# Reordering the side jobs of an expert chunk: the place of two weight loads among three float64 pieces

## The chip, the cores and the metric

The kernel runs on one core of a Trainium2 chip. The metric is device time in microseconds (us), the median of several executions.

## What is computed

Three stages follow one another on 2304 tokens with 512 features: windowed attention, a mixture of eight experts whose gate is normalised by rows and columns, and a dense layer pair with a leaky ReLU. The weights `w_in` and `w_out` of the last pair arrive as float64.

```python
scores = np.where(mask, scale * q @ k.T + bias, -1e9)     # 4 x 8 heads, 576 tokens, window 128
x = softmax(scores) @ v                                   # (2304, 512)
P = exp(x @ w_gate - max);  8 times: P /= P.sum(1); P /= P.sum(0); P *= N / E
for e in range(8):                                        # D = 512, F = 1024
    out += P[:, e:e+1] * (np.maximum(x @ w1[e], 0) @ w2[e])
h = out @ w_in                                            # d_ff = 2048, float64 weights
return np.maximum(0.01 * h, h) @ w_out
```

## The kernel before

**Chunks and units.** Each expert's hidden layer is cut into two halves, so there are 16 expert chunks, followed by 4 chunks of the dense pair. A chunk has two weight matrices of 512 x 512, which the code calls factors: `W[0][ci]` (from `w1`) and `W[1][ci]` (from `w2`). A chunk is worked off in five units, one for each group of token tiles, in the order 0, 4, 1, 2, 3. Each matrix product is done with seven block products instead of eight (a Strassen scheme), in float16 parts. In every unit TensorE runs the steps of the first product (`a_steps`, L707, results `s` and `sq`) mixed with those of the second product of the unit before (`b_steps`, L824, results `t`). ScalarE and VectorE empty the PSUM banks: L719 and L731 (ScalarE, to `q`), L723 (VectorE, to `sq`), L755, L761 and L777 (ScalarE, to the float16 `h`), L736 (VectorE), L834 (ScalarE, to `part`), L835 (GpSimd, `part` into `acc`), L837 (VectorE, `t` into `acc`). TensorE can only go on with a bank when the reader of its last content is done.

**Side jobs.** While chunk ci is computed, the factors of chunk ci+1 have to be loaded and prepared. For each factor there is one load of 1 MB (L551, on SP's queue), then `scale()`: four ScalarE passes that find the size of its numbers (`largest`, L555), a short chain over TensorE and VectorE for the scale, four ScalarE passes that apply it (L558); then `early()`: the first two float16 parts (L429 on ScalarE, L430 on GpSimd) and four sums (L582, GpSimd). Besides, the float64 weights of the last stage are turned to float32 in 32 pieces, three of them in each of the expert chunks 1 to 10 and two in chunk 11. A piece is a load of 512 KB (L630), then five jobs: `exponent` (L636 VectorE, L639 ScalarE), `signed` (L642 VectorE), `high` (L647 VectorE, L648 ScalarE), `low` (L654 ScalarE, L656 GpSimd), `put` (L660 GpSimd, then the store L661 on SP's queue).

**What sets the order.** The jobs are functions in the list `side`, filled when unit 4 of a chunk begins (`p == 4`). After each TensorE step `tick` takes one or two from the list's front; a `None` is a step without a job. The number taken is such that the list is empty at the end of the chunk. A scheduler then places the instructions on each engine, where they run in order. All large loads, of factors and pieces, share the tile tag `raw` with two buffers (8 KB in each partition): a load has to wait until the buffer's last user is done, which for a piece is the landing of its store. SP's queue issues in order.

In the job list before, all pieces stand ahead of both factors: load piece 1, load piece 2, piece 1, load piece 3, piece 2, piece 3, load both factors, ten empty steps, `scale` and `early` of the first factor, then of the second.

Of the kernel before, what the change touches and what calls it, by code (L numbers as in the profile page):

```python
# [31 lines left out]
def attn_moe_kernel(  # L32
# [81 lines left out]
    side, gating, inputs = [], [], []  # L114
# [18 lines left out]
    def tick(n=1):  # L133
        for d in due:
            d[0] -= 1
        for d in [d for d in due if d[0] <= 0]:
            due.remove(d)
            d[1]()
        pop(gating)
        pop(inputs)  # L140
        for _ in range(n):
            pop(side)
# [291 lines left out]
    def weigh_pair(ci, p):  # L434
        t0, n = PAIRS[p]
        if ci not in pu:
            pu[ci] = small.tile([P, NTILE], F32, tag="pu", name="pu")
        c = slice(t0, t0 + 2 * n)
        nc.scalar.activation(out=pu[ci][:, c], in_=rxt[0 if ci == 0 else 1][:, c], func=AF.Copy, scale=rw[ci])

    class Inputs:
# [22 lines left out]
        def weigh(self):  # L464
            c = slice(self.t0, self.t0 + 2 * self.n)
            nc.scalar.activation(out=rxt[self.phase][:, c], in_=self.sr[:, 1:2].to_broadcast([P, 2 * self.n]), func=AF.Copy)
            if self.phase == 0:
                weigh_pair(0, self.p)
# [64 lines left out]
    NCE = len(chunks)  # L533
    for c in range(F2 // FC):
        chunks.append((win32[:, c * FC:(c + 1) * FC], wout32[c * FC:(c + 1) * FC, :], None))
    NC = len(chunks)
# [73 lines left out]
    def weights(ci):  # L610
        for which in range(2):
            W[which][ci] = Weights(ci, which)
# [237 lines left out]
    def merge(a, b):  # L850

        if not b:
            return a
        seq = [a[0], b[0], a[1], a[2], b[1]] + a[3:7]
        a, b = a[7:], b[2:]
        tail = b[-3:] if len(b) > 10 else b[-1:]
        b = b[:len(b) - len(tail)]
        na, nb = 0, 0
        while na < len(a) or nb < len(b):
            if nb < len(b) and nb * len(a) <= na * len(b):  # L860
                seq.append(b[nb])
                nb += 1
            else:
                seq.append(a[na])
                na += 1
        return seq + tail
# [93 lines left out]

    cast = list(range(2 * KT * (F2 // FC)))

    def cast_jobs(n):

        todo = [to_single(cast.pop(0)) for _ in range(min(n, len(cast)))]
        jobs = [load for load, _ in todo[:2]] + [None] * 8
        for k, (_, rest) in enumerate(todo):
            jobs += rest + [load for load, _ in todo[k + 2:k + 3]]
        return jobs

    def weight_jobs(ci):
        weights(ci)
        a, b = W[0][ci], W[1][ci]
        return [a.load, b.load] + [None] * 10 + a.scale() + a.early() + b.scale() + b.early()

    def weigh(ci):
        pu[ci] = small.tile([P, NTILE], F32, tag="pu", name="pu")
# [12 lines left out]
    for n, u in enumerate(units + [None]):  # L990
        a, b = [], b_steps(*prev)
        if u is not None:
            ci, p = u
            assert ci < NCE or p in split_pairs
            a = a_steps(ci, p)
            k0 = len(a) - 7
            if p == ends[ci] and ci + 1 < NC:
                a = [[f] + ([lambda j=k - k0: W[0][ci + 1].at(j)] if k >= k0 else []) for k, f in enumerate(a)]
            else:
                a = [[f] for f in a]  # L1000
        if prev[1] == ends[prev[0]] and prev[0] + 1 < NC:
            k0 = len(b) - 7
            b = [[f] + ([lambda j=k - k0: W[1][prev[0] + 1].at(j)] if k >= k0 else []) for k, f in enumerate(b)]
        else:
            b = [[f] for f in b]
        if u is not None and ci >= 1:
            if n and units[n - 1][0] != ci and ci != NCE:
                weigh(ci)
            if p == 4:
                side += cast_jobs(3) if ci < NCE - 1 else []  # L1010
                side += weight_jobs(ci + 1) if ci + 1 < NC else []
        if prev[0] == NCE:
            weigh_pair(*prev)
        seq = merge(a, b) if a else b

        rest = {4: 57, 1: 36, 2: 8, 3: -19}.get(p) if u is not None and ci >= 1 else None
        for k, fs in enumerate(seq):
            for f in fs:
                f()
            if u is not None and ci == 0:  # L1020
                tick(2)
            elif u is None or not side:
                tick()
            elif rest is not None:
                tick(-(-len(side) // max(len(seq) - k + rest, 1)))
            else:
                tick()
        assert u is None or p != 3 or not side
        if prev[0] == NCE - 1:
            inputs += [None] * 6 + Inputs(prev[1], 1).all()  # L1030
        if u == (1, 0):
            assert not any(gating)
        prev = u
# [43 lines left out]
```

## Time and profile before

| | |
|---|---|
| median of 3 runs (lowest, highest) | 2003.38 us (2001.25, 2008.05) |
| profiled execution, first to last instruction | 2015.9 us |
| TensorE busy | 1911.6 us (95%) |
| VectorE, ScalarE, GpSimd busy | 1408.6 us (70%), 1365.7 us (68%), 1319.5 us (65%) |
| mean granted clock of TensorE | 0.984 |

The page gives no other time for the profiled execution than its span, which lies 0.6% above the median of the runs. All places below are counted from the span's start; chunk 7, which is followed closely, runs from about 850 to 940 us. A busy TensorE may still be slow: the granted clock says whether its matmuls run at full speed (1.0) or half (0.5).

### The profile page before, as it was taken

The page shows a single profiled execution, that of the slowest core. Times are in us where ns is not written, and L with a number is a line of the kernel's source. Part 1 is how long each engine was busy: PE and PEld are TensorE (multiplying, and loading weights), DVE is VectorE, ACT ScalarE, POOL GpSimd, SP SyncE. Part 2 cuts the span into 40 slices and gives each one's busy share as a digit, 9 for nine tenths or more (in the row PEclk, how much of TensorE's full clock was granted, in tenths as well). Part 3 has the DMA queues.
Part 4 walks back from the last instruction along what each step waited for, and adds up shares of the span by engine and source line. Part 5 has one row for each costly group of instructions (what it writes and reads, how often), then busy time and mean ns, then how long its engine had stood idle before and what let it go on. Part 6 is the DMA issues. An engine that isn't in the chain of part 4 may idle for free.

```text
span 2015.9 us, 45342 instructions
## 1 busy us (share of the span) xinstructions
PE 1911.6 (95%) x17693; PEld 1654.9 (82%) x17693; DVE 1408.6 (70%) x3881; ACT 1365.7 (68%) x3110; POOL 1319.5 (65%) x1133
## 2 busy tenths in 40 slices
PE   8899988899999989999999999999999998999998
PEld 6677767788888878788887888889898887889897
DVE  5877568666767767676766677666666677677776
ACT  6776685767666666757666675766666678776754
POOL 4632346577685868677685877767657686667743
PEclk9799899999999999999999999999999999999999
DMA  4231000111202021111202021100010000001002
GB/s 126 79 90 48 22 7 22 69 38 58 68 28 80 22 69 38 54 64 38 79 12 79 22 69 54 43 22 30 15 43 23 22 22 22 22 22 43 1 22 74
DMA packets 55271, 88.90 MB, mean 44 GB/s; under 512 B 3344, under 2 KB 21776, under 8 KB 55056
## 3 DMA queue, kind: packets, MB, share of 16 engines
q1 hardware_dynamic: 55056, 86.01, 13.1%
q8 instruction: 138, 2.26, 0.5%
q14 instruction: 77, 0.63, 0.1%
HBM read 72.89 MB, written 13.11 MB: 43 GB/s over the span
## 4 chain that ended last, share of the span: by engine, by line
PE 73%; DVE 9%; ACT 6%; DMA 4%; POOL 4%; issue 3%; SPq 0%; POOLq 0%; ACTq 0%; DVEq 0%
PE t L824 33%; PE s L707 20%; PE sq L707 14%; PE s L234 3%; DMA raw<-in_moe_w_dram 3%; PE o L288 2%; PE pt L273 2%; DVE e L262 1%; DVE acc L837 1%; ACT junk L555 1%; DVE raw L642 1%; POOL h L780 1%; DVE h L736 1%; DVE s L736 1%; POOL acc L835 1%
## 5 line engine op out<-in xcount | busy, mean ns | idle before, releaser
L824 PE MATMUL t<-w,h 128*128 128x256 f16 x7560 | 978.0, 274 | 37.2 <-ACT part L834 14.4
L707 PEld LDWEIGHTS <-w 128*128 128x128 f16 x8400 | 761.0, 98 | 129.5 <-issue 42.5
L824 PEld LDWEIGHTS <-h 128*128 128x128 f16 x7560 | 732.3, 98 | 143.6 <-issue 44.6
L707 PE MATMUL s<-xp,w 128*128 128x256 f16 (+1 forms) x4908 | 618.4, 264 | 34.4 <-ACT q L731 23.3
L837 DVE SCALAR_TENSOR_TENSOR acc<-t,pu,acc 128x256 f32<-128x256 f32 x864 | 406.7, 478 | 238.7 <-PE t L824 193.2
L780 POOL TENSOR_TENSOR h<-s,h 128x1024 f16<-128x1024 f32 x180 | 386.7, 2149 | 181.5 <-ACT h L777 133.6
L707 PE MATMUL sq<-xp,w 128*128 128x256 f16 (+1 forms) x3492 | 439.5, 262 | 2.0 <-ACT q L719 1.0
L835 POOL TENSOR_TENSOR acc<-acc,part 128x256 f32<-128x256 f32 x324 | 242.0, 749 | 240.8 <-ACT part L834 177.0
L430 POOL TENSOR_TENSOR w<-raw,w 128x512 f16<-128x512 f32 x240 | 277.8, 1175 | 46.8 <-ACT w L429 46.5
L736 DVE SCALAR_TENSOR_TENSOR h<-sq,h 128x512 f16<-128x512 f32 (+1 forms) x348 | 190.7, 549 | 68.5 <-ACT h L761 50.8
L834 ACT ACTIVATE part<-t,pu 128x256 f32<-128x256 f32 x324 | 152.7, 471 | 118.7 <-PE t L824 109.1
L777 ACT ACTIVATE h<-s 128x1024 f16<-128x1024 f32 x180 | 190.0, 1055 | 47.1 <-DVE s L736 44.3
L723 DVE SCALAR_TENSOR_TENSOR sq<-sq,q 128x256 f32<-128x256 f32 x348 | 148.4, 427 | 78.2 <-PE sq L707 67.5
L719 ACT ACTIVATE q<-s 128x256 f32<-128x256 f32 x366 | 138.5, 381 | 84.5 <-PE s L707 60.8
L429 ACT ACTIVATE w<-raw 128x512 f16<-128x512 f32 x240 | 147.5, 626 | 15.1 <-PE t L824 7.9
L736 DVE SCALAR_TENSOR_TENSOR s<-sq,s 128x256 f32<-128x256 f32 x348 | 144.1, 414 | 2.6
L755 ACT ACTIVATE h<-sq 128x512 f16<-128x512 f32 x174 | 103.5, 595 | 55.1 <-DVE sq L723 31.9
L736 DVE SCALAR_TENSOR_TENSOR s<-sq,q 128x256 f32<-128x256 f32 x348 | 129.9, 414 | 11.8 <-ACT q L731 9.8
L723 DVE SCALAR_TENSOR_TENSOR sq<-s,q 128x256 f32<-128x256 f32 x174 | 74.6, 429 | 88.5 <-ACT q L719 80.6
L555 ACT ACTIVATE junk<-raw 128x512 bf16<-128x512 f32 x160 | 100.6, 629 | 31.8 <-DMA raw<-in_moe_w_dram 30.9
L558 ACT ACTIVATE raw<-raw,sr 128x512 f32<-128x512 f32 x160 | 102.3, 714 | 1.5 <-DVE sr L424 1.4
L582 POOL TENSOR_TENSOR raw<-raw 128x512 f32<-128x512 f32 x80 | 102.5, 1281 | 0.0
(139 smaller groups left out, 1867.6 us busy)
## 6 DMA issues: line engine op xcount, KB each, us to landing
raw<-in_moe_w_dram SPq DMA_DIRECT2D x32, 1024.0 KB, 5.2
raw<-in_moe_w_in_dram SPq DMA_DIRECT2D x16, 512.0 KB, 3.7
raw<-in_moe_w_out_dram SPq DMA_DIRECT2D x16, 512.0 KB, 3.5
q_t<-in_q_dram SPq DMA_DIRECT2D x18, 256.0 KB, 3.2
k_t<-in_k_dram SPq DMA_DIRECT2D x18, 256.0 KB, 3.0
v_t<-in_v_dram SPq DMA_DIRECT2D x18, 256.0 KB, 2.8
out_dram<-acc SPq DMA_DIRECT2D x18, 256.0 KB, 2.0
win<-raw SPq DMA_DIRECT2D x16, 256.0 KB, 2.4
```

Source lines behind the costliest of these rows:

```text
L429: nc.scalar.activation(out=hi, in_=src, func=AF.Copy)
L430: nc.gpsimd.tensor_tensor(out=lo, in0=src, in1=hi, op=ALU.subtract)
L707: nc.tensor.matmul(d[b][:, f, :], t[:, wp, kk, ft * P:(ft + 1) * P], XP[p][:, o, kk, xp, :], start=(i == 0 and f == 0 and j in FIRST), sto ...
L719: nc.scalar.activation(out=q[:, k], in_=ps, func=AF.Copy, scale=CS)
L723: nc.vector.scalar_tensor_tensor(out=block(k), in0=ps, scalar=CS, in1=q[:, k], op0=ALU.mult, op1=ALU.add)
L736: nc.vector.scalar_tensor_tensor(out=out, in0=in0, scalar=sc, in1=in1, op0=op0, op1=op)
L777: nc.scalar.activation(out=h[:, 3:7, 0, :], in_=d["s"], func=AF.Copy)
L780: nc.gpsimd.tensor_tensor(out=h[:, 3:7, 1, :], in0=d["s"], in1=h[:, 3:7, 0, :], op=ALU.subtract)
L824: nc.tensor.matmul(ps, h[:, o, hp, f, tt * P:(tt + 1) * P], w[:, wp, ft, :], start=(i == 0 and j in FIRST), stop=(i == 5), skip_group_chec ...
L834: nc.scalar.activation(out=part, in_=ps, func=AF.Copy, scale=s)
L835: nc.gpsimd.tensor_tensor(out=dst, in0=dst, in1=part, op=ALU.add)
L837: nc.vector.scalar_tensor_tensor(out=dst, in0=ps, scalar=s, in1=dst, op0=ALU.mult, op1=ALU.add)
```

## The change

`cast_jobs` and `weight_jobs` become one function, `side_jobs`. In a chunk with three pieces its list is: load piece 1, load piece 2, eight empty steps, piece 1, **load first factor**, piece 2, load piece 3, four empty steps, **`scale` of the first factor**, piece 3, **load second factor**, `early` of the first, eight empty steps, `scale` and `early` of the second. The amount of work is the same; the list is two steps longer (85 entries instead of 83). Where there are only two pieces (chunk 11) the second factor is loaded behind the second piece. Where there are none (chunks 12 and on) the list is as before.

```diff
-    def cast_jobs(n):
+    def side_jobs(ci, n):
 
         todo = [to_single(cast.pop(0)) for _ in range(min(n, len(cast)))]
-        jobs = [load for load, _ in todo[:2]] + [None] * 8
-        for k, (_, rest) in enumerate(todo):
-            jobs += rest + [load for load, _ in todo[k + 2:k + 3]]
-        return jobs
-
-    def weight_jobs(ci):
         weights(ci)
         a, b = W[0][ci], W[1][ci]
-        return [a.load, b.load] + [None] * 10 + a.scale() + a.early() + b.scale() + b.early()
+        jobs = [load for load, _ in todo[:2]]
+        if not todo:
+            return [a.load, b.load] + [None] * 10 + a.scale() + a.early() + b.scale() + b.early()
+        jobs += [None] * 8 + todo[0][1] + [a.load]
+        if len(todo) > 1:
+            jobs += todo[1][1]
+        if len(todo) > 2:
+            jobs += [todo[2][0]] + [None] * 4 + a.scale() + todo[2][1] + [b.load] + a.early()
+        else:
+            jobs += [b.load] + [None] * 8 + a.scale() + a.early()
+        return jobs + [None] * 8 + b.scale() + b.early()
...
             if p == 4:
-                side += cast_jobs(3) if ci < NCE - 1 else []
-                side += weight_jobs(ci + 1) if ci + 1 < NC else []
+                side += side_jobs(ci + 1, 3 if ci < NCE - 1 else 0) if ci + 1 < NC else []
```

On SP's queue the eight DMAs of such a chunk stand in this order before: load 1, load 2, store 1, load 3, store 2, first factor, store 3, second factor. In the changed kernel: load 1, load 2, store 1, first factor, store 2, load 3, store 3, second factor.

The order of instructions moves at three places of chunk 7 that matter below. Buffer numbers are part of the names: `raw_11959`, `raw_11961` are pieces 1 and 2 in both kernels; piece 3 is `raw_12097` before and `raw_12138` in the changed kernel; the first factor is `raw_12205` before and `raw_12077` in the changed one.

VectorE, around the last VectorE job of piece 1 (L647), before:

```order
L723 SCALAR_TENSOR_TENSOR sq_11971<-s0_11945,q_11944 128x256
L723 SCALAR_TENSOR_TENSOR sq_12217<-sq_12217,q_12196 128x256
L642 SCALAR_TENSOR_TENSOR raw_11959<-raw_11959,sign_88 128x512
L837 SCALAR_TENSOR_TENSOR acc15_116<-t0_11836,pu_10394,acc15_116 128x256
L736 SCALAR_TENSOR_TENSOR h_11943<-sq_11971,h_11943 128x2x256
L723 SCALAR_TENSOR_TENSOR sq_12008<-sq_12008,q_11944 128x256
L647 TENSOR_SCALAR raw_11959<-raw_11959 128x512
```

The same place of the changed kernel:

```order
L642 SCALAR_TENSOR_TENSOR raw_11959<-raw_11959,sign_88 128x512
L837 SCALAR_TENSOR_TENSOR acc15_116<-t0_11836,pu_10394,acc15_116 128x256
L723 SCALAR_TENSOR_TENSOR sq_11971<-s0_11945,q_11944 128x256
L647 TENSOR_SCALAR raw_11959<-raw_11959 128x512
L723 SCALAR_TENSOR_TENSOR sq_12008<-sq_12008,q_11944 128x256
```

L647 now follows directly on the L723 that closes a block product of unit 4; before, three other instructions stood between the sign job and it.

ScalarE, from the L755 of the first half of unit 1 on, before:

```order
L755 ACTIVATE h_12195<-sq_12217 128x2x256
L648 ACTIVATE raw_11961<-raw_11961,ones_90 128x512
L834 ACTIVATE part_12143<-t1_12136,pu_11680 128x256
L761 ACTIVATE h_12195<-sq_12242 128x256
L731 ACTIVATE q_12196<-s0_12197 128x256
L654 ACTIVATE raw_12097<-raw_12097 128x512
L719 ACTIVATE q_12288<-s0_12289 128x256
L639 ACTIVATE raw_12097<-raw_12097,shift_92 128x512
L834 ACTIVATE part_12164<-t2_12157,pu_11680 128x256
```

The same place of the changed kernel:

```order
L755 ACTIVATE h_12192<-sq_12214 128x2x256
L555 ACTIVATE junk_12181,mxw_11940<-raw_12077 128x512
L834 ACTIVATE part_12147<-t1_12140,pu_11680 128x256
L555 ACTIVATE junk_12190,mxw_11940<-raw_12077 128x512
L555 ACTIVATE junk_12202,mxw_11940<-raw_12077 128x512
L761 ACTIVATE h_12192<-sq_12243 128x256
L731 ACTIVATE q_12193<-s0_12194 128x256
L555 ACTIVATE junk_12212,mxw_11940<-raw_12077 128x512
L719 ACTIVATE q_12302<-s0_12303 128x256
L834 ACTIVATE part_12164<-t2_12157,pu_11680 128x256
```

The four passes over the first factor (L555) now stand here, one of them ahead of the first L834; the jobs of pieces 2 and 3 that stood here have moved ahead and behind.

GpSimd, from the first job of piece 1 on, before:

```order
L656 TENSOR_TENSOR raw_11959<-raw_11959 128x512
L835 TENSOR_TENSOR acc2_103<-acc2_103,part_12093 128x256
L660 TENSOR_TENSOR raw_11959<-raw_11959 128x512
L780 TENSOR_TENSOR h_11943<-s_12070,h_11943 128x4x256
L656 TENSOR_TENSOR raw_11961<-raw_11961 128x512
L835 TENSOR_TENSOR acc1_102<-acc1_102,part_12143 128x256
L660 TENSOR_TENSOR raw_11961<-raw_11961 128x512
L835 TENSOR_TENSOR acc3_104<-acc3_104,part_12164 128x256
L780 TENSOR_TENSOR h_12195<-s_12275,h_12195 128x4x256
L656 TENSOR_TENSOR raw_12097<-raw_12097 128x512
L660 TENSOR_TENSOR raw_12097<-raw_12097 128x512
```

In the changed kernel, from the second job of piece 2 on (in piece 1 the L660 likewise follows directly on its L656):

```order
L656 TENSOR_TENSOR raw_11961<-raw_11961 128x512
L660 TENSOR_TENSOR raw_11961<-raw_11961 128x512
L835 TENSOR_TENSOR acc1_102<-acc1_102,part_12147 128x256
L835 TENSOR_TENSOR acc3_104<-acc3_104,part_12164 128x256
L780 TENSOR_TENSOR h_12192<-s_12286,h_12192 128x4x256
L835 TENSOR_TENSOR acc16_117<-acc16_117,part_12240 128x256
L835 TENSOR_TENSOR acc17_118<-acc17_118,part_12330 128x256
L656 TENSOR_TENSOR raw_12138<-raw_12138 128x512
L780 TENSOR_TENSOR h_12301<-s_12398,h_12301 128x4x256
L660 TENSOR_TENSOR raw_12138<-raw_12138 128x512
```

Pieces 1 and 2 have lost the L835 that stood inside them, and piece 3 stands two L835 later and has an L780 inside.

## Rows read from the trace of the kernel before

**Rows 1.** TensorE groups, 400 to 1205 us: count, busy, mean ns, idle before, releasers.

```profile
L824 PE MATMUL t<-w,h 128*128 128x256 f16 x3408 | 436.0, 274 | 15.3 <-ACT part L834 10.6 <-DVE acc L837 4.3 <-POOL h L780 0.2
L707 PE MATMUL s<-xp,w 128*128 128x256 f16 (+1 forms) x2157 | 272.3, 265 | 21.6 <-ACT q L731 20.3 <-ACT q L719 0.8 <-DVE sq L723 0.4
```

**Rows 2.** Stretches: chunks 2 to 10, and chunk 13, which has no float64 pieces.

```profile
core 0: us, PE busy (x) PEld busy (x) DVE busy (x) ACT busy (x) POOL busy (x), PEclk, DMA share, GB/s
400.00:1205.30 805.30, 768.33 (x7221) 674.97 (x7220) 549.86 (x1388) 541.74 (x1177) 594.45 (x500) 0.99 0.16 51
1361.80:1446.30 84.50, 84.50 (x813) 75.39 (x811) 55.73 (x148) 55.27 (x123) 57.12 (x50) 1.00 0.08 26
```

**Rows 3.** Waits, 300 to 1300 us: in total, times, longest.

```profile
ACT junk L555 <- DMA raw<-in_moe_w_dram: 30.9, 16, 4.4
```

**Rows 4.** Timeline of SP's queue, chunk 7: start, us, DMA issued.

```profile
891.36 0.33 SPq L661 DMA_DIRECT2D wout<-raw  x1
...
900.06 0.33 SPq L661 DMA_DIRECT2D wout<-raw  x1
902.19 0.38 SPq L551 DMA_DIRECT2D raw<-in_moe_w_dram  x1
```

**Rows 5.** Timeline of ScalarE, chunk 7, at five places.

```profile
896.47 0.46 ACT L834 ACTIVATE part<-t,pu 128x256 f32<-128x256 f32 x1
...
904.83 0.47 ACT L834 ACTIVATE part<-t,pu 128x256 f32<-128x256 f32 x1 [0.61 <-PE t L824]
907.20 0.63 ACT L555 ACTIVATE junk<-raw 128x512 bf16<-128x512 f32 x1 [1.90 <-DMA raw<-in_moe_w_dram]
...
908.84 0.37 ACT L731 ACTIVATE q<-s 128x256 f32<-128x256 f32 x1
...
923.26 1.04 ACT L777 ACTIVATE h<-s 128x1024 f16<-128x1024 f32 x1
```

**Rows 6.** Timeline of TensorE, chunk 7; idle time before in brackets.

```profile
895.53 0.81 PE L824 MATMUL t<-w,h 128*128 128x256 f16 x6
896.98 0.81 PE L824 MATMUL t<-w,h 128*128 128x256 f16 x6 [0.64 <-ACT part L834]
...
909.27 2.52 PE L707 MATMUL s<-xp,w 128*128 128x256 f16 x12 [2.25 <-ACT q L731]
```

**Rows 7.** Timeline of TensorE, the same stall in chunks 2 and 4.

```profile
464.25 0.81 PE L824 MATMUL t<-w,h 128*128 128x256 f16 x6 [3.03 <-ACT part L834]
...
726.89 0.81 PE L824 MATMUL t<-w,h 128*128 128x256 f16 x6 [3.28 <-ACT part L834]
```

**Rows 8.** Stretches behind the stall of chunk 7; columns as in rows 2.

```profile
909.27:912.85 3.58, 3.58 (x18) 2.58 (x18) 2.25 (x8) 3.02 (x8) 1.21 (x2) 0.53 0.76 208
917.00:940.00 23.00, 23.00 (x210) 20.02 (x208) 14.54 (x44) 18.64 (x42) 16.99 (x15) 1.00 0.00 1
```

**Rows 9.** Instructions on the tile raw: duration in ns, least, median, most.

```profile
L647 DVE TENSOR_SCALAR raw<-raw x32: 406/410/2214, 339.0 to 1248.6; 128x512 int32<-128x512 int32 x32
L648 ACT ACTIVATE raw<-raw,ones x32: 706/722/733, 340.2 to 1250.2; 128x512 f32<-128x512 int32 x32
L656 POOL TENSOR_TENSOR raw<-raw x32: 1277/1292/1398, 350.0 to 1254.2; 128x512 f32<-128x512 f32 x32
L660 POOL TENSOR_TENSOR raw<-raw x32: 1262/1272/1362, 352.0 to 1255.6; 128x512 f32<-128x512 f32 x32
```

**Rows 10.** Costliest groups of the whole run, from the page.

```profile
L723 DVE SCALAR_TENSOR_TENSOR sq<-sq,q 128x256 f32<-128x256 f32 x348 | 148.4, 427 | 78.2 <-PE sq L707 67.5
L755 ACT ACTIVATE h<-sq 128x512 f16<-128x512 f32 x174 | 103.5, 595 | 55.1 <-DVE sq L723 31.9
L780 POOL TENSOR_TENSOR h<-s,h 128x1024 f16<-128x1024 f32 x180 | 386.7, 2149 | 181.5 <-ACT h L777 133.6
```

**Rows 11.** Timeline of GpSimd, chunk 7, the add of acc17.

```profile
910.54 0.73 POOL L835 TENSOR_TENSOR acc<-acc,part 128x256 f32<-128x256 f32 x1 [3.04 <-PE s L707]
```

**Rows 12.** DMA from issue to landing, us: the loads of L551.

```profile
DMA to landing us min/median/max: 4.9/5.2/10.1
```

## The prediction

> **What bounds the kernel now.** I read the groups of TensorE first, then stretches, then the waits and the timelines of one chunk. In chunks 2 to 10, which take 805.3 us, TensorE is busy for 768.3 us; in chunk 13, which has no float64 pieces, it never idles [rows 2]. So TensorE is the bound, and the nine chunks with three pieces lose 37.0 us to idle time. The reader should see how few causes that has: 21.6 us lie ahead of matmuls into `s`, 20.3 of them until ScalarE's L731, and 15.3 us ahead of matmuls into `t`, 10.6 of them until ScalarE's L834 [rows 1].
>
> Both releasers are ScalarE, which has idle time of its own, so the question is what ScalarE waited for. Its first pass over a new factor (L555) waited 30.9 us for the factor's load, in 16 waits of up to 4.4 us [rows 3]. Chunk 7 shows how this reaches TensorE. ScalarE is through with L834 at 905.3, finds the factor not there and stands until 907.20; two passes and L761 later L731 starts, at 908.84; TensorE has waited 2.25 us for it when it goes on at 909.27 [rows 5, 6]. In chunks 2 and 4 the same late factor shows as an L834, with 3.03 and 3.28 us [rows 7]. I count as the DMA stall of the nine chunks 20.3 + 3.0 + 3.3 = 26.6 us, 3.0 a chunk. The other 10.4 us, 1.15 a chunk, are short waits such as the 0.64 us at 896.98 [rows 6].
>
> Why is the factor late? Its load is issued at 902.19, when the store of piece 2, issued at 900.06, has landed: the store costs 2.1 us, the load 5.0 (to 907.20) [rows 4, 5]. Piece 1's store went out at 891.36 [rows 4], nearly 11 us earlier, but its buffer was given to piece 3.
>
> There is a second loss behind the stall. From 909.27 to 912.85 the granted clock is 0.53 and TensorE needs 3.58 us for 18 matmuls, 199 ns each; later it is 1.00 and 23.0 us hold 210, 110 ns each [rows 8]. These are the levels of 1.2 and 2.4 GHz; before the fall TensorE had stood idle for 2.25 us. Such a spell costs 18 x 89 ns = 1.6 us. Over the nine chunks the mean clock is 0.99, so about 8 us of 805 go this way (4 to 12, given the rounding) [rows 2].
>
> **The change, part by part.** The instructions are the same; the code orders both the work and SP's DMAs anew. I follow chunk 7 and take its times for all nine, since their pattern repeats.
>
> *First factor, earlier load.* It now waits for piece 1's store. When does that go out? L647 of piece 1 stands directly behind the L723 that closes a block product of unit 4. In the changed order 105 matmuls of 256 columns and 24 of 128 lie between that product and the `t0` group that starts at 895.53 [rows 6]; at 110 ns, and half of it, these take 12.9 us, so the product ends at 882.7. Then follow, one behind the other, L723 0.43, L755 0.60 (beside it L647, 0.41), L648 0.72, L656 1.29 and L660 1.27, with nothing between them any more [rows 9, 10]: the store is issued at about 887.1, 4.3 us earlier than now. It lands at 889.2, the factor at 894.2 to 894.4.
>
> *First factor, earlier use.* The first L555 now stands where ScalarE used to do piece 2's L648, ahead of the L834 that ran at 896.47 [rows 5]. The product whose reading that place follows ends 42 matmuls before 895.53, at 890.9; L723 and L755 take 1.0 [rows 10], so ScalarE gets there at about 892. So it still waits for the load, about 2 us as today, but at another place. What is queued behind it: L834, two more passes, L761, L731. L555 runs 894.3 to 894.9 and L834 until 895.4, and TensorE wants L834 only at 895.53 + 6 x 0.11 = 896.2 [rows 6]: no stall, where there are 0.64 us now. Two passes and L761 take 1.64 us as they do at 907.20 [rows 5], so L731 runs 897.0 to 897.4, and TensorE, which wants it at 896.85, loses 0.55; a further pass delays an L719 by about 0.5. That is 1.05 us against 1.15 today. But the load can be slower than the 5.0 us: the median of this line's loads is 5.2 and single ones take more [rows 12]. I take 0.2 a chunk more than today: +1.8 us.
>
> *The old place.* At 905 piece 3 takes the place of the four passes. Its load follows the landing of piece 2's store, and piece 2 has also moved forward, so VectorE and ScalarE find it there. The DMA stall goes: -26.6 us. Cover gone would mean piece 3 late instead, at most the same stall.
>
> *Second factor, later load.* It now waits for piece 3's store, and on GpSimd piece 3 stands behind the L835 of acc17, now at 910.54 [rows 11]. Without the stall and the slow spell this is 3.9 us earlier, 906.6, done at 907.4; L656, one L780 (2.15) and L660 bring it to 912.1 [rows 9, 10], the store to 914.2, the load to 919.4. ScalarE wants it behind an L777 that now begins at 923.26 [rows 5], so at 924.3 - 3.9 = 920.4. That is 1 us to spare, and TensorE does not want the next L719 at once. Bounds: nothing, or, if GpSimd waits for the L777 that feeds its L780, some 2 us a chunk. I take 0.5, nearer to the row: +4.5 us.
>
> *The clock.* Stalls of 2 us and more vanish, so I take 7 of the 8 us back.
>
> *Nothing for the rest.* Chunk 11, with two pieces, and chunk 1, where the gate runs too, I count at nothing, though they have stalls as well; two empty steps hide under TensorE's own work, as the list still ends with the chunk. The other stages keep their order.
>
> Sum: -26.6 + 1.8 + 4.5 - 7.0 = -27.3 us. The profiled execution took 2015.9 and would take 1988.6; it is 0.6% above the median of the runs, and the stalls are in both, so I carry the difference over: 2003.4 - 27.3 = 1976 us.
>
> **A rule on the clock.** The row shows a slow spell behind a stall of 2.25 us [rows 6, 8]. The Trainium skill, "TensorE: Matmul & The Clock Gate", Part 1, says that the hardware judges activity in a window that runs freely, so that how many matmuls are slow differs from run to run. By the rows the term is -7; by the rule it depends on where a gap falls and could be anything from 0 to -8. The trace has both cases only in so far as the mean of 0.99 is less than a spell in each chunk would give.
>
> **The rivals.**
> - *The clock gives nothing back.* The remaining short waits could still meet slow spells. Then the sum is -20.3: 1983 us. What the Trainium skill says of the free-running window ("TensorE: Matmul & The Clock Gate", Part 1) allows this.
> - *The second factor becomes the late one.* If its load lands 3 us later than worked out, ScalarE stands for about 2 us in each chunk; TensorE loses those instead of the 0.5: +13.5 us, and the clock term goes. -26.6 + 1.8 + 18 = -6.8: 1997 us. For it speaks the chain of three GpSimd steps, store and load; against it that ScalarE now gets rid of piece 3 before.
> - *The wait has only moved.* If the first factor lands 2 us later than worked out (896.3), L834 and L731 are late by 1.4 to 2 us and the old stall stands at the new place: about 2003, no change.
> - *Slower.* If piece 1's store goes out no earlier than now, at 891.36, the factor lands at 898.5, 4.2 us later than worked out; TensorE then loses 1.05 + 3.6 = 4.7 us there against the 4.15 of today, and every chunk meets a slow spell: nine times 0.5 + 1.6, less the 8 of today, + 4.5 for the second factor: +15, so 2018 us. It decides from a landing at about 897.3. Against it: the order on VectorE and GpSimd has cleared the way of piece 1.
>
> That the change does nothing is excluded: SP's queue has the factor ahead of store 2.
>
> **How the numbers follow.** I give 0.51 to the forecast (1966 to 1987), 0.12 to the clock's case (1983), 0.15 to the second factor (1997), 0.11 to a wait that only moves (2003), 0.11 to slower (2010 and up). What a measurement here can tell from no change is about 0.3%, 6 us. Faster is forecast, clock's case, and most of the third: 0.76; same 0.13; slower 0.11. The range from 1963 to 2003 leaves out the slower cases and a little below, where all stalls vanish (-37 - 8 = -45 would be 1958).
>
> **What would show it.** In the new profile the wait of TensorE for L731 in chunks 2 to 10 falls from 20.3 us to under 8; store 1 of chunk 7 goes out near 887, the factor's load directly behind it; L555's first wait on its load is about 2 us and ahead of an L834; the second factor's wait is near 0; chunks take 86 to 87 us, not 89.5. I am wrong if piece 1 is not earlier (VectorE's other work may hold its jobs back), or if the second L555 of a chunk waits for more than 2 us.

## The result, and the profile after

The changed kernel takes 1973.56 us (median of 4 runs, 1969.18 to 1977.06), the kernel before 2005.72 us in runs taken beside it: a ratio of 0.983 (95% interval 0.980 to 0.986). The forecast was 1976 us, in a range from 1963 to 2003. The profiled execution has a span of 1975.3 us, 40.6 us less than the one of before.

The groups of TensorE in chunks 2 to 10, which now run from 396.1 to 1168.6 us (against [rows 1]; columns as there):

```profile
L824 PE MATMUL t<-w,h 128*128 128x256 f16 x3408 | 441.4, 273 | 2.9 <-ACT part L834 1.8 <-DVE acc L837 0.9
L707 PE MATMUL s<-xp,w 128*128 128x256 f16 (+1 forms) x2165 | 272.5, 262 | 9.5 <-ACT q L731 8.7 <-DVE sq L723 0.3
L707 PE MATMUL sq<-xp,w 128*128 128x256 f16 (+1 forms) x1620 | 211.5, 262 | 0.7 <-ACT q L719 0.7
```

The same nine chunks, and chunk 13, as stretches (against [rows 2]):

```profile
396.10:1168.60 772.50, 759.34 (x7229) 671.64 (x7227) 547.10 (x1390) 544.54 (x1173) 591.04 (x497) 1.00 0.16 53
1320.30:1403.80 83.50, 83.50 (x804) 74.51 (x802) 54.09 (x146) 54.39 (x121) 57.37 (x49) 1.00 0.08 27
```

The nine chunks take 772.5 us instead of 805.3. Two things make up the 32.8: TensorE's idle time falls from 37.0 to 13.2 us (772.50 - 759.34), and its busy time for the same work from 768.3 to 759.3, because the stretch now runs at a granted clock of 1.00. The other 7.8 us of the span's difference lie outside: 2.7 in chunk 11 (86.1 to 83.4 us), 3.3 in the first 300 us, where nothing was changed, the rest in small pieces. The medians differ by 32.2 us, so some 8 of the 40.6 belong to these two executions and not to the kernels.

ScalarE's waits for a factor's load, in total, times, longest, from 300 to 1270 us (against [rows 3]):

```profile
ACT junk L555 <- DMA raw<-in_moe_w_dram: 40.0, 20, 2.9
```

This is the surprise: they have not become shorter. There were 30.9 us in 16 waits; now there are 40.0 in 20. In the nine chunks the first passes over a first factor wait 20.5 us in 9 waits (20.1 in 8 before), those over a second factor 17.7 in 9 (5.3 in 5 before). What TensorE loses and what ScalarE waits for have come apart. Chunk 7 shows how. It begins at 828.0 instead of 850.3, so 22.3 us are to be added to compare a place with before.

SP's queue in chunk 7 (against [rows 4]):

```profile
864.35 0.33 SPq L661 DMA_DIRECT2D wout<-raw  x1
866.42 0.38 SPq L551 DMA_DIRECT2D raw<-in_moe_w_dram  x1
...
890.52 0.33 SPq L661 DMA_DIRECT2D wout<-raw  x1
892.59 0.38 SPq L551 DMA_DIRECT2D raw<-in_moe_w_dram  x1
```

ScalarE at the two places where a factor is first used, in the brackets the idle time before (against [rows 5]):

```profile
871.51 0.63 ACT L555 ACTIVATE junk<-raw 128x512 bf16<-128x512 f32 x1 [2.28 <-DMA raw<-in_moe_w_dram]
...
872.14 0.46 ACT L834 ACTIVATE part<-t,pu 128x256 f32<-128x256 f32 x1
...
874.13 0.37 ACT L731 ACTIVATE q<-s 128x256 f32<-128x256 f32 x1
...
895.15 1.05 ACT L777 ACTIVATE h<-s 128x1024 f16<-128x1024 f32 x1
897.65 0.63 ACT L555 ACTIVATE junk<-raw 128x512 bf16<-128x512 f32 x1 [1.46 <-DMA raw<-in_moe_w_dram]
```

TensorE at the same two places (against [rows 6]):

```profile
872.06 1.47 PE L824 MATMUL t<-w,h 128*128 128x256 f16 x12
874.55 1.70 PE L707 MATMUL s<-xp,w 128*128 128x256 f16 x12 [1.02 <-ACT q L731]
...
897.24 0.82 PE L707 MATMUL sq<-xp,w 128*128 128x256 f16 x6
897.89 0.27 PE L707 MATMUL s<-xp,w 128*128 128x256 f16 x1
```

ScalarE stands 2.28 us for the first factor, a little longer than the 1.90 of before, but TensorE has other products in hand meanwhile and loses 1.02 us where it lost 2.25. At the second factor ScalarE stands 1.46 us and TensorE has no idle time at all. The other chunks agree. The gaps of TensorE that end within 3.3 us of the start of a first factor's late pass add up to 22.3 us before and to 9.4 now; behind the second factor's they are 0.3 and 0.7 us.

One long stall is left, in chunk 1: there ScalarE waits for the load of a float64 piece with an L834 right behind it, and TensorE loses 3.04 us, after which the granted clock is 0.50 from 366.1 to 371.0. ScalarE there:

```profile
365.01 0.67 ACT L654 ACTIVATE raw<-raw 128x512 f32<-128x512 uint32 x1 [2.79 <-DMA raw<-in_moe_w_in_dram]
365.58 0.45 ACT L834 ACTIVATE part<-t,pu 128x256 f32<-128x256 f32 x1
```

and TensorE:

```profile
366.09 1.44 PE L824 MATMUL t<-w,h 128*128 128x256 f16 x6 [3.04 <-ACT part L834]
```

### The profile page after: what moved, and what is told of

It is laid out like the page before. It is cut to its first block, busy times and chain, and to the rows that moved or that the text cites. A ratio compares the mean times of both kernels' runs of the same rounds, so it can differ in the third digit from the quotient of the medians.

```text
span 1975.3 us, 45321 instructions
## 1 busy us (share of the span) xinstructions
PE 1899.9 (96%) x17693; PEld 1650.3 (84%) x17693; DVE 1401.9 (71%) x3881; ACT 1370.4 (69%) x3110; POOL 1320.1 (67%) x1133
## 4 chain that ended last, share of the span: by engine, by line
PE 75%; DVE 7%; ACT 6%; DMA 5%; POOL 4%; issue 2%; SPq 0%; POOLq 0%; ACTq 0%; DVEq 0%
PE t L824 34%; PE s L707 20%; PE sq L707 14%; DMA raw<-in_moe_w_dram 3%; PE s L234 3%; PE o L288 2%; PE pt L273 2%; DVE e L262 1%; ACT junk L555 1%; POOL h L780 1%; DVE s L736 1%; POOL w L430 1%; ACT raw L558 1%; DVE acc L837 1%; ACT e L250 1%
## 5 line engine op out<-in xcount | busy, mean ns | idle before, releaser
L837 DVE SCALAR_TENSOR_TENSOR acc<-t,pu,acc 128x256 f32<-128x256 f32 x864 | 407.1, 478 | 219.5 <-PE t L824 168.7
L780 POOL TENSOR_TENSOR h<-s,h 128x1024 f16<-128x1024 f32 x180 | 388.5, 2158 | 132.3 <-ACT h L777 92.8
L707 PE MATMUL sq<-xp,w 128*128 128x256 f16 (+1 forms) x3492 | 446.8, 262 | 3.3 <-ACT q L719 1.7
L835 POOL TENSOR_TENSOR acc<-acc,part 128x256 f32<-128x256 f32 x324 | 236.3, 731 | 284.5 <-ACT part L834 246.9
L834 ACT ACTIVATE part<-t,pu 128x256 f32<-128x256 f32 x324 | 152.9, 472 | 110.5 <-PE t L824 102.0
L777 ACT ACTIVATE h<-s 128x1024 f16<-128x1024 f32 x180 | 189.6, 1053 | 43.0 <-DVE s L736 41.7
L723 DVE SCALAR_TENSOR_TENSOR sq<-sq,q 128x256 f32<-128x256 f32 x348 | 148.2, 426 | 64.5 <-PE sq L707 52.1
L719 ACT ACTIVATE q<-s 128x256 f32<-128x256 f32 x366 | 138.7, 380 | 71.3 <-PE s L707 58.4
L755 ACT ACTIVATE h<-sq 128x512 f16<-128x512 f32 x174 | 103.2, 593 | 59.0 <-PE t L824 28.7
L723 DVE SCALAR_TENSOR_TENSOR sq<-s,q 128x256 f32<-128x256 f32 x174 | 74.4, 428 | 81.7 <-ACT q L719 76.7
L555 ACT ACTIVATE junk<-raw 128x512 bf16<-128x512 f32 x160 | 100.2, 626 | 41.1 <-DMA raw<-in_moe_w_dram 40.0
L761 ACT ACTIVATE h<-sq 128x256 f16<-128x256 f32 x174 | 66.1, 380 | 66.4 <-DVE sq L723 59.4
```

Source lines behind the costliest of these rows:

```text
L707: nc.tensor.matmul(d[b][:, f, :], t[:, wp, kk, ft * P:(ft + 1) * P], XP[p][:, o, kk, xp, :], start=(i == 0 and f == 0 and j in FIRST), sto ...
L719: nc.scalar.activation(out=q[:, k], in_=ps, func=AF.Copy, scale=CS)
L723: nc.vector.scalar_tensor_tensor(out=block(k), in0=ps, scalar=CS, in1=q[:, k], op0=ALU.mult, op1=ALU.add)
L777: nc.scalar.activation(out=h[:, 3:7, 0, :], in_=d["s"], func=AF.Copy)
L780: nc.gpsimd.tensor_tensor(out=h[:, 3:7, 1, :], in0=d["s"], in1=h[:, 3:7, 0, :], op=ALU.subtract)
L834: nc.scalar.activation(out=part, in_=ps, func=AF.Copy, scale=s)
```

## The experiments

Twelve kernels were run. In the first expectations A is the theory that the earlier load brings the gain, B its rival; from the fifth on each says anew what its letters stand for. All ratios are to the kernel before, run beside each.

**The load alone, in the list.** The first factor is loaded behind piece 1 as in the change, but stays in the list where it was scaled before.

```diff
         if len(todo) > 2:
-            jobs += [todo[2][0]] + [None] * 4 + a.scale() + todo[2][1] + [b.load] + a.early()
-        else:
-            jobs += [b.load] + [None] * 8 + a.scale() + a.early()
-        return jobs + [None] * 8 + b.scale() + b.early()
+            jobs += [todo[2][0]] + todo[2][1]
+        return jobs + [b.load] + [None] * 10 + a.scale() + a.early() + b.scale() + b.early()
```

> One part of the change alone: the first factor is loaded behind piece 1 (so it waits for store 1), but it is scaled behind piece 3 and ten empty steps, as before. Theory A (the gain comes from which store the load waits for): the first pass over the first factor waits 0, TensorE's idle time in chunks 2 to 10 falls from 37 to about 15 us (1.15 a chunk that were there anyway, 0.5 for two passes ahead of L731), the slow-clock spells go: 1970 to 1980 us, like the changed kernel. Rival B (the gain comes from scaling the first factor early, which spreads the work of ScalarE and GpSimd): idle stays above 30 us, 1995 to 2005 us.

Measured: 2005.86 us, 1.001 (0.999 to 1.003). This edit gives nothing. A fell; of B the idle time held (37.3 us), the time lies a little above its range. But the run does not show the load alone. In its chunk 7 the scheduler has drawn the four passes ahead of piece 3, although the list has them behind it: the first pass stands 48.4 us behind the start of a chunk (median of the nine), against 56.9 in the kernel before and 43.9 in the change. So the passes are early here too, and piece 3, whose load now stands behind the factor's, is the late one. ScalarE's timeline at its first pass:

```profile
890.02 0.63 ACT L555 ACTIVATE junk<-raw 128x512 bf16<-128x512 f32 x1 [1.62 <-DMA raw<-in_moe_w_dram]
```

VectorE's at the first job of piece 3:

```profile
897.27 0.43 DVE L636 TENSOR_SCALAR raw<-raw 128x512 int32<-128x512 int32 x1 [2.05 <-DMA raw<-in_moe_w_out_dram]
```

TensorE's behind that:

```profile
898.48 0.22 PE L404 MATMUL mt<-identb,e 128*1 128x128 bf16 x1 [1.36 <-DVE acc L837]
900.38 1.44 PE L824 MATMUL t<-w,h 128*128 128x256 f16 x6 [1.68 <-ACT part L834]
```

VectorE waits 2.05 us for piece 3 with an L837 behind; TensorE wants that L837, then an L834, and loses 1.36 + 1.68 = 3.04 us, as much as a chunk of before lost to the factor. The prediction had this as "Cover gone would mean piece 3 late instead, at most the same stall".

**The place alone, in the list.** The change, with the loads of piece 3 and of the first factor exchanged, so that SP's order is that of before.

```diff
-        jobs += [None] * 8 + todo[0][1] + [a.load]
+        jobs += [None] * 8 + todo[0][1] + ([todo[2][0]] if len(todo) > 2 else [a.load])
...
-            jobs += [todo[2][0]] + [None] * 4 + a.scale() + todo[2][1] + [b.load] + a.early()
+            jobs += [a.load] + [None] * 4 + a.scale() + todo[2][1] + [b.load] + a.early()
```

> The changed kernel with two entries of the list exchanged: the load of piece 3 stands behind piece 1, and that of the first factor behind piece 2, so that it waits for store 2 again; all else, with the early scaling, is as in the changed kernel. Theory A: the factor lands some 8 us later than in the changed kernel, ScalarE waits longer than 2.3 us for it and TensorE's idle time comes back: 1990 to 2030 us. Rival B: the early scaling does it, 1970 to 1980 us.

Measured: 1984.12 us, 0.989 (0.987 to 0.992): two thirds of the gain, with the load behind store 2 as before. Neither range held it. This run does not show the early place alone either. The scheduler has put the passes back: the first stands 54.1 us behind the start of a chunk (median), 10 us later than in the change and 3 earlier than before, and its load is issued at 48.4 (51.9 before, 38.8 in the change). So two thirds of the gain came with the passes nearly where they had been, and with waits for loads of 25.8 us instead of 39.3. The idle time that is left has another place: half of the 23.3 us that TensorE idles in the nine chunks lies ahead of the small matmuls of the scale chain, which follow the fourth pass (group of TensorE):

```profile
L404 PE MATMUL mt<-identb,e 128*1 128x128 bf16 x18 | 4.0, 220 | 11.6 <-DVE e L398 11.6
```

**Eight empty steps instead of four** ahead of the first factor's scaling.

```diff
-            jobs += [todo[2][0]] + [None] * 4 + a.scale() + todo[2][1] + [b.load] + a.early()
+            jobs += [todo[2][0]] + [None] * 8 + a.scale() + todo[2][1] + [b.load] + a.early()
```

> The changed kernel with eight empty steps instead of four between the load of piece 3 and the scaling of the first factor. The remaining wait of L555 for its load (about 2.3 us a chunk) falls below 0.5 us. If the 1.0 us that TensorE still idles a chunk at that place comes from the two passes ahead of L731, as theory A has it, it stays between 0.5 and 1.0 us and the time is 1968 to 1975 us. If the load's wait itself makes it, 9 us go: 1962 to 1966 us.

Measured: 2007.31 us, 1.002 (0.999 to 1.004). The whole gain is gone, which neither theory had. The first factor's waits were to fall below 0.5 us a chunk; they are 14.2 us in seven of the nine chunks. One stall, that of the second factor in chunk 6, on ScalarE:

```profile
824.42 0.63 ACT L555 ACTIVATE junk<-raw 128x512 bf16<-128x512 f32 x1 [2.43 <-DMA raw<-in_moe_w_dram]
...
825.80 0.36 ACT L731 ACTIVATE q<-s 128x256 f32<-128x256 f32 x1
```

The same on TensorE:

```profile
822.93 0.49 PE L824 MATMUL t<-w,h 128*128 128x256 f16 x3
826.22 0.81 PE L707 MATMUL s<-xp,w 128*128 128x256 f16 x6 [2.79 <-ACT q L731]
```

ScalarE's wait is 2.43 us here, and TensorE loses 2.79. The second factor of chunk 6 waits nearly as long in the change, 2.18 us until 812.57, and TensorE loses nothing there. The difference is what TensorE has to do. Here L731 stands behind two passes, and TensorE runs out with the group at 822.93, while the pass still waits. There it runs without a gap from 806 to 817. The first factor of the change in chunk 7 lies between: TensorE has work until 873.53, two microseconds beyond the wait's end, and loses 1.02.

**Two passes more.** Two further ScalarE passes over the first factor (their results are not used) ahead of the four.

```diff
+        def extra(self, n):
+            for k in range(n):
+                junk = stg.tile([P, FC], BF16, tag="junk", bufs=1, name="junk")
+                nc.scalar.activation(out=junk, in_=self.raw[:, k], func=AF.Square)
...
-            jobs += [todo[2][0]] + [None] * 4 + a.scale() + todo[2][1] + [b.load] + a.early()
+            jobs += [todo[2][0]] + [None] * 4 + [lambda: a.extra(2)] + a.scale() + todo[2][1] + [b.load] + a.early()
```

> The changed kernel with two more passes (0.63 us each, results not used) of ScalarE over the first factor ahead of its four, in each of the ten chunks with three pieces. Theory A: TensorE has under 1 us to spare for L834 at that place and none for L731, so the two passes, 1.3 to 1.6 us, come out at TensorE nearly whole: idle +10 to +15 us, 1984 to 1992 us, and some slow-clock spells may come back. Rival C (ScalarE's time at that place is covered by its idle time, only the place of the old stall was not): +0 to +4 us, 1973 to 1978 us.

Measured: 1997.6 us, 0.996 (0.995 to 0.998). Its lines are numbered five higher; neither range held the time. The groups of TensorE show that the loss has spread over both releasers:

```profile
L829 PE MATMUL t<-w,h 128*128 128x256 f16 x3394 | 440.4, 273 | 13.9 <-ACT part L839 9.6 <-DVE acc L842 4.1
L712 PE MATMUL s<-xp,w 128*128 128x256 f16 (+1 forms) x2154 | 273.2, 262 | 12.3 <-ACT q L736 11.9
```

The dose is no clean one: nine times two passes of 0.63 us are 11 us, and 24 are lost, with an order that is new on every engine.

**Without the store in the chain.** The waiting itself can be changed without touching the list: L660 writes its product into a small tile, from which it is stored, so that the large buffer is free when L660 ends and no longer when the store has landed (the load that waits for it was issued 2.07 us behind the store).

```diff
-            nc.gpsimd.tensor_tensor(out=man, in0=man, in1=d["fac"].bitcast(F32), op=ALU.mult)
-            nc.sync.dma_start(dst, man)
+            out = stg.tile([P, FC], F32, tag="t2", name="out32")
+            nc.gpsimd.tensor_tensor(out=out, in0=man, in1=d["fac"].bitcast(F32), op=ALU.mult)
+            nc.sync.dma_start(dst, out)
```

In the kernel before:

> The kernel before with one edit: the last job of a piece (L660) writes its product into a small tile of its own and the store reads that, so that the piece's large buffer is free when L660 ends and no longer when the store has landed (2.1 us earlier). Theory A (what the first users wait for their loads is what TensorE loses): the waits of first users in chunks 2 to 10 fall from 39 us to about 20, TensorE's idle time there from 37 to about 18, time about 1980. Theory A' (the scheduler puts each first user about 2 us ahead of the landing wherever the load is, and TensorE pays only where it needs the waiting engine at that moment): the waits stay at 30 to 42 us; the idle time follows from what stands behind each wait, so the time may be anywhere from 1975 to 2010.

In the changed kernel:

> The changed kernel with the same edit. Theory A: waits of first users from 41 to about 22 us, TensorE's idle time in chunks 2 to 10 from 13 to about 6, time 1962 to 1968. Theory A': waits stay at 35 to 42, idle time of 8 to 30, time 1968 to 1995.

Measured: 1986.65 us (0.989, 0.986 to 0.992) and 1967.1 us (0.979, 0.976 to 0.982). A' fell: the waits of first users in the nine chunks are 17.7 us instead of 39.3, and 20.2 instead of 41.3. A's numbers were near: TensorE's idle time is 23.2 instead of 37.0 us (about 18 expected), and 7.6 instead of 13.2. The second of these has the lowest median of the study, but its 6 us under the change are little more than the scatter of the runs (1961.39 to 1973.66 us, against 1969.18 to 1977.06). SP's queue in its chunk 7:

```profile
860.25 0.33 SPq L662 DMA_DIRECT2D wout<-out  x1
860.69 0.38 SPq L551 DMA_DIRECT2D raw<-in_moe_w_dram  x1
```

ScalarE's first pass over that factor:

```profile
865.98 0.62 ACT L555 ACTIVATE junk<-raw 128x512 bf16<-128x512 f32 x1
```

Its nine chunks as a stretch:

```profile
397.50:1160.50 763.00, 755.41 (x7217) 670.63 (x7216) 547.71 (x1387) 544.73 (x1171) 590.04 (x496) 1.00 0.17 54
```

The factor's load is issued 0.44 us behind the store, not 2.07, and the first pass finds it there.

**Without the scheduler.** Each engine runs its instructions in the order of the code.

```diff
-    with _tile.TileContext(nc, schedule_with_timeline_sim=True) as tc:
+    with _tile.TileContext(nc, schedule_with_timeline_sim=False) as tc:
```

In the kernel before:

> The kernel before without the scheduler: every engine runs its instructions in the order in which the code lists them. The span will be longer as a whole; what counts is chunks 2 to 10 beside those of listed_after. Theory A: the late factor is a matter of the list, so these chunks lose some 20 to 30 us more here than in listed_after. Theory A': the list leaves ten empty steps and the second factor's load between the first load and its first pass, so first users hardly wait (under 15 us in all) and the nine chunks differ by less than 10 us from those of listed_after.

In the changed kernel:

> The changed kernel without the scheduler. Theory A: chunks 2 to 10 are 20 to 30 us shorter than in listed_before. Theory A': they differ by less than 10 us, either way, and the first users' waits are under 15 us in both.

Measured: 2226.35 us (1.108, 1.103 to 1.113) and 2234.98 us (1.113, 1.108 to 1.117). The nine chunks are longer with the change, 919.2 us against 902.0. That is against A, and the second theory's 10 us were also too few. TensorE's group of `t` in listed_before:

```profile
L824 PE MATMUL t<-w,h 128*128 128x256 f16 x3391 | 465.4, 278 | 96.7 <-DVE acc L837 74.8 <-ACT part L834 11.9 <-POOL h L780 8.2
```

The same group in listed_after:

```profile
L824 PE MATMUL t<-w,h 128*128 128x256 f16 x3393 | 470.3, 280 | 104.7 <-DVE acc L837 64.0 <-POOL h L780 39.3
```

ScalarE's waits for factors in listed_before:

```profile
ACT junk L555 <- DMA raw<-in_moe_w_dram: 5.4, 7, 1.3
```

and in listed_after:

```profile
ACT junk L555 <- DMA raw<-in_moe_w_dram: 15.6, 9, 2.0
```

In list order the factor was hardly late before (5.4 us of waits), and the change makes it later (15.6), while L780 on GpSimd holds TensorE up for 39.3 us instead of 8.2. All first users together wait 15.7 and 15.6 us, just over the 15 of the second theory. So the list is not better by itself; the gain belongs to the order that the scheduler makes of it.

**Lists next to it.** Two and six empty steps where the change has four.

```diff
-            jobs += [todo[2][0]] + [None] * 4 + a.scale() + todo[2][1] + [b.load] + a.early()
+            jobs += [todo[2][0]] + [None] * 2 + a.scale() + todo[2][1] + [b.load] + a.early()
```

> The changed kernel with two empty steps instead of four ahead of the first factor's scaling. If the time follows the place of the passes smoothly (four steps 1974, eight 2007), this is 1960 to 1985. Rival (the scheduler orders all engines anew for each list, and neighbouring lists scatter): anything from 1970 to 2010, with first users' waits of 30 to 42 us in chunks 2 to 10 whatever the time.

> The changed kernel with six empty steps instead of four. Smooth: between four and eight, 1985 to 1998. Rival (scatter between neighbouring lists): as likely below 1980 or above 2000, and waits of 30 to 42 us.

Measured: 1990.97 us (0.992, 0.990 to 0.995) and 1992.98 us (0.993, 0.991 to 0.995). Two steps missed the smooth range and lie in the rival's, with waits of 48.6 us outside of its 30 to 42; six steps lie in the smooth range. With 2, 4, 6 and 8 steps the kernel takes 1991, 1974, 1993 and 2007 us: four is a good spot, with losses on both sides of it. Four points fit a narrow valley as well as scatter; for scatter speaks that the idle time lies elsewhere each time. (The profile of six_steps is of its slowest run, 2001.91 us.) Ahead of `t` in two_steps:

```profile
L824 PE MATMUL t<-w,h 128*128 128x256 f16 x3418 | 442.7, 273 | 14.0 <-ACT part L834 13.3 <-DVE acc L837 0.5
```

and in six_steps, where VectorE's L837 has as large a part as L834:

```profile
L824 PE MATMUL t<-w,h 128*128 128x256 f16 x3396 | 439.8, 273 | 15.2 <-ACT part L834 7.9 <-DVE acc L837 7.2
```

**The store out of the chain of two bad lists.** The edit of staged_after in the kernel of eight_steps and in that of load_only:

> The kernel of eight_steps (eight empty steps ahead of the first factor's scaling instead of four, 2007 us) with the small tile for the store as in staged_after. Theory A'' (TensorE loses the length of a first user's wait, times a share that depends on what stands behind the waiting instruction): the waits of first users in chunks 2 to 10 fall from 36 us to 16 to 22, TensorE's idle time there from 36.5 to 15 to 23, time 1980 to 1992. Rival (the order of the instructions alone sets the loss, the length of the wait does not): idle time stays above 30 us and the time above 1998.

> The kernel of load_only (first factor loaded behind piece 1, but scaled at the old place of the list, 2006 us) with the small tile for the store. Theory A'' (the store's 2.1 us come off every wait for a load behind it, and TensorE is paid back by the share of the waits that is exposed, 37 of 41 us in load_only): the waits of first users in chunks 2 to 10 fall from 41 to about 20 us, TensorE's idle time from 37 to 16 to 22, time 1980 to 1990. Rival (the early scaling is needed for any gain): idle time above 28, time above 1995.

Measured: 1974.24 us (0.985, 0.982 to 0.987) and 1987.26 us (0.990, 0.988 to 0.993). Both become faster, by 33 and 19 us, so the rivals fell. But the account of A'' does not hold either. In staged_eight the time came out below its range, with 28.9 us of waits where 16 to 22 were expected. In staged_load_only the time came out in its range, but the waits grew from 41.5 to 53.2 us, where about 20 were expected, while TensorE's idle time fell from 37.3 to 23.4. TensorE's group of `t` there (lines one higher), where load_only had 19.8 us:

```profile
L825 PE MATMUL t<-w,h 128*128 128x256 f16 x3400 | 437.3, 273 | 15.4 <-ACT part L835 11.1 <-DVE acc L838 3.6
```

ScalarE's waits for factors there, as many and in total as long as in load_only (27.8 us in 15):

```profile
ACT junk L555 <- DMA raw<-in_moe_w_dram: 27.8, 15, 4.1
```

**All kernels with the scheduler**, chunks 2 to 10. "Waits" adds the waits for loads of L555, L636 and L654 (in two_extra_passes of the lines that answer to them); "idle" is the stretch less TensorE's busy time:

| kernel | waits, us | idle, us | median, us |
|---|---|---|---|
| before | 39.3 | 37.0 | 2005.72 |
| after | 41.3 | 13.2 | 1973.56 |
| load_only | 41.5 | 37.3 | 2005.86 |
| swap_loads | 25.8 | 23.3 | 1984.12 |
| two_steps | 48.6 | 23.5 | 1990.97 |
| six_steps | 31.3 | 26.8 | 1992.98 |
| eight_steps | 36.0 | 36.2 | 2007.31 |
| two_extra_passes | 41.2 | 29.5 | 1997.60 |
| staged_before | 17.7 | 23.2 | 1986.65 |
| staged_after | 20.2 | 7.6 | 1967.10 |
| staged_eight | 28.9 | 14.4 | 1974.24 |
| staged_load_only | 53.2 | 23.4 | 1987.26 |

The median follows the idle column closely. It does not follow the waits: four kernels with 39 to 42 us of them have idle times from 13 to 37 us.

## Why the prediction was right, and where it was not

**First factor, earlier load.** Store 1 was forecast at 887.1 and went out at 864.35 + 22.3 = 886.65; the load was to land at 894.2 to 894.4, and the pass that waits for it begins at 871.51 + 22.3 = 893.81. The chain from the L723 over L647, L648, L656 and L660 was read rightly.

**First factor, earlier use.** Forecast: a wait of 2 us ahead of an L834, no stall at that L834, and 1.05 us lost, 0.55 at L731 and 0.5 at L719. Measured in chunk 7: 2.28 us of wait, none lost at L834, 1.02 at L731. Over the nine chunks L731 holds TensorE up for 8.7 us, 0.97 a chunk, so the mark "under 8" was missed by a little: the loss is that of the forecast, but nearly all of it at L731. In chunk 7 L731 and TensorE's need for it both came earlier than worked out, by 0.6 and 1.0 us.

**The old place.** The term of -26.6 us for the DMA stall was right as to TensorE: the 20.3 us at L731 are gone, since the 8.7 are those of the new place, and `t` has fallen from 15.3 to 2.9 us. Its reason was too narrow. Not all of it was the first factor: TensorE's gaps behind that factor's late passes are 22.3 us, and the 2.45 us of chunk 3 stand behind a late piece (ScalarE, then TensorE, in the trace of before):

```profile
538.26 0.67 ACT L654 ACTIVATE raw<-raw 128x512 f32<-128x512 uint32 x1 [1.94 <-DMA raw<-in_moe_w_in_dram]
540.59 0.99 PE L707 MATMUL s<-xp,w 128*128 128x256 f16 x5 [2.45 <-ACT q L731]
```

The 3.28 us at 726.89 lie in chunk 5, and not in chunk 4 as [rows 7] has it.

**Second factor, later load.** The load was well forecast (store 3 at 912.1, measured 912.8; use 919.95, forecast landing 919.4). The need was not: ScalarE was through with L777 at 895.15 + 1.05 + 22.3 = 918.5, not 920.4, and waits 1.46 us where "near 0" was forecast. Over the nine chunks these waits are 17.7 us, 1.96 a chunk, and in chunks 2, 5 and 6 they are 2.54, 2.47 and 2.18 us: taking "the second L555 of a chunk" for the second factor's first pass, over 2 us was named as a sign of being wrong. So ScalarE's half of the rival "The second factor becomes the late one" came true. Its other half did not: TensorE lost 0.7 us behind all nine. The prediction had noted that TensorE does not want the next L719 at once, but for a wait of about nothing; that this held for 2 us was luck. The term of +4.5 us should have been under 1; with it the forecast of idle time was 16.7 us (37.0 - 26.6 + 1.8 + 4.5), and 13.2 came.

**The clock.** Forecast -7.0, measured -9.0 (768.33 to 759.34 of busy time for the same work). No wait of TensorE in the nine chunks is now longer than 1.10 us. That a long wait doesn't always bring a spell is in the trace of before: behind 2.25 us the granted clock is 0.53 [rows 8], and behind the 3.03 us at 464.25 [rows 7] it is 1.00 (columns as in [rows 2]):

```profile
464.25:467.85 3.60, 3.60 (x34) 3.23 (x34) 2.09 (x7) 3.44 (x9) 1.87 (x2) 1.00 0.38 77
```

The Trainium skill, "TensorE: Matmul & The Clock Gate", Part 1, says that the window in which the hardware judges activity runs freely, so that the number of slow matmuls varies. These two places fit that, but no run here shows the window.

**Counted at nothing.** Chunk 1 rightly (99.6 to 99.3 us), chunk 11 not: 2.7 us.

**The sum** for the nine chunks was -27.3 us and came out at -32.8: 3.5 more from idle time, where the second factor's 4.5 were not lost, and 2.0 more from the clock. A chunk takes 85.8 us, a little under the 86 to 87 of the forecast. The medians differ by 32.2 us, 4.9 more than the sum; the time of 1976 us came nearer, because it was counted from 2003.4 and the kernel before took 2005.72 beside the change.

**What the runs correct** is the reason behind the sum. The prediction asked "Why is the factor late?", and took the lateness for the cause. The rows show that ScalarE waits for the first factor as long as ever (20.1 us before, 20.5 now), while TensorE's gaps behind these waits fall from 22.3 to 9.4 us. What has changed is where the wait falls: one of 2.3 us costs TensorE 1.0 us where it has matmuls in hand for 2 us beyond it, and one of 2.4 us costs it 2.8 where they run out during the wait. The prediction did see this place in the order of the changed kernel and worked the loss out from it, which is why the number came right. From the list alone it could not have been right: eight_steps differs from the change by four empty steps, fits every sentence of its argument on the loads, and gains nothing.

What share of the gain the load has and what share the place is not shown. As entries of the list the load alone gave nothing and the place alone two thirds, but in what ran load_only has the passes early too, and swap_loads has them nearly at the old place.

Taking the store's landing out of the chain made the kernel faster in four pairs, by 19 to 33 us in three of them; in the fourth, the change itself, the 6 us are little more than the scatter of the runs. How much of a shorter chain is paid back, and whether the waits shrink, depends on the order that the scheduler then makes; why a given list gets the order it gets was not settled, since no run holds the order fixed while a wait is changed.

## What to carry to other kernels

A wait costs what the bounding engine lacks while it lasts, so price a moved wait at its new place, from the order of that kernel: how many instructions the bounding engine has left that need nothing from the waiting one. Where a scheduler orders the engines anew for each list, a reordering that gains is worth a few neighbours before one believes in its reason; here two empty steps more or less took away over half of it, and four more all. A change that shortens the chain itself, such as freeing a buffer before its store has landed, helped by 19 to 33 us in three of the four lists that it was put into, and did not hurt in the fourth.

## What was not expected of the hardware

- Idle time and half clock are loosely tied. Two_steps idles for 23.5 us in its nine chunks, with one wait of 2.40 us, and its mean granted clock there is 1.00; in the kernel before a wait of 2.25 us brought 0.53 [rows 6, 8].
- The same edit (the small tile for the store) changed what ScalarE waited for a factor by -8.4, -23.8, -12.4 and 0 us in the four kernels (25.4 to 17.0, 38.2 to 14.4, 29.9 to 17.5, 27.8 to 27.8), though it took the landing of the store out of the chain in all four.
